# Operand addresses, PSUM banks, the start of the program and the order tables changed in an attention and two-MoE kernel

## The chip, the cores and the metric

The kernel runs on one core of a Trainium2 chip. The metric is the device time of one execution in microseconds (us); lower is better. The median of three timed runs of the kernel before is 945.14 us, with 944.86 and 945.75 as the lowest and the highest. One further execution was profiled; every row below comes from it. Engines are named as in the profile: PE (matmul), PEld (weight load), DVE (vector), ACT (scalar), POOL, SP (starts the DMAs).

## The reference, cut to what matters

```python
# q, k, v: 4 batches x 8 heads x 576 x 64; omega: 128 x 64; x becomes 2304 x 512
def phi(x):                                   # x: q or k, scaled by D ** -0.25
    h = einsum('bhsd,md->bhsm', x, omega) - sum(x * x, -1, keepdims=True) / 2
    return exp(h - max(h, -1)) / sqrt(128)
kv = einsum('bhsm,bhsd->bhmd', phi(k), v);  z = sum(phi(k), 2)
attn = einsum('bhsm,bhmd->bhsd', phi(q), kv) / (phi(q) . z + 1e-6)
x = attn rearranged to 2304 tokens x 512
h = maximum(x @ w_in, 0);  x = (h * h) @ w_out              # moe:  512 -> 2048 -> 512
xn = x / sqrt(mean(x * x) + 1e-6) * rms_g                    # moe2: 512 -> 1536 -> 512
g = xn @ w_gate;  out = (silu(g) * (xn @ w_val)) @ w_out
```

## The kernel before, in words

The work is cut into tokens blocks of 512 columns, one for each of the four batches, and a remainder block (REM) of 4 x 64 tokens that is 256 columns wide. Attention of a batch runs as four pairs of heads. Features (line 661) multiply 64-row halves of the array (form 64*128); products with values and with the kv state (lines 706, 720, 723, 780, 785, 810) use 64-column halves (128*64); transposes (774, 819) use the whole array, as do all large matmuls. The first MoE is `moe1(j)`: for each of 16 chunks of the hidden dimension `hpart` (line 895) multiplies x by w_in into a bank of class `h`, ACT and others form the squared relu, and `ypart` (line 926) adds the product with w_out into four banks that stay accumulating. The second MoE uses `product` (line 1204) and lines 1306, 1326 and 1400. Large matmuls hold fp32r values split in a high and a low part and take three products for each one; each instruction has 512 columns (256 for REM). The program holds 3162 such matmuls of 512 columns and 672 of 256.

Every piece of work is a node in `Plan`, with an engine, a planned duration and the buffers that it reads and writes. `Plan.run` (lines 286 to 312) issues the nodes one after the other in the sequence of the table ORDER. Its words are two bytes: the node's number and, in the top four bits, which of its alternative engines it takes. The word 0xFFFF issues a filler instead (lines 562 to 567): two 256-column matmuls of `ones` by `ones` into an accumulator bank that nobody reads. The table PLACES gives, for each buffer acquired, its class and slot. Work is issued in this order to each engine's own queue, and each engine runs its queue in order, waiting where data or a buffer is missing. DMAs run on SP's queue by `dma` (line 470).

PSUM has eight banks in three classes: `t` (three), `h` (one), `acc` (four). A buffer names the classes that it may take; `banks` in `attention` is `["t"]` for batches 1 to 3. SBUF tiles come from pools; `const`, then `common`, are allotted from one side, `edge` and the attention pool from the other. The weights of moe1 are split once, by `prepare`, during moe1(0), and parts are kept in DRAM (`w1d`).

At the start, ones are set by DVE, fillers begin on PE, and omega is loaded twice (the two 64-row halves), scaled by ACT at line 573 to `oms`, and the row norms of q, k and the remainder are formed (lines 584, 615). Line 668 takes the maxima of features from PSUM on DVE, line 680 the exponentials on ACT.

Of the kernel before, what the change touches and what calls it, by code (L numbers as in the profile page):

```python
# [21 lines left out]


ORDER = bytes.fromhex(
    "000000150005101600170001000400070014ffffffffffffffffffffffffffffffffffffffffffffffffffffffffffff0019"
    "0003002120220023004f0020ffffffffffffffffffffffffffff00240072107320500051001a001b0009000a001c001d001e"
    "001fffffffffffffffffffff000d004e00250074002600270028100b0029004400450043000e000fffffffffffffffffffff"
    "ffffffffffffffffffffffffffffffff0047002a0030000c003600100011001300080012007d0046007e0031004200520048"
    "0049004a004b007f0053004d007c0037004c002e102f00540018002b0180018300a0002c102d0055005c0181005600580057"
    "00801182105d019100710081008201ae10a10059005a00ab009f01840083105b008400860032003301920038003900640185"  # L30
    "00e50065003a003400aa005e009e00cd01a1005fffffffff0075018601af0085119301b01187003b003500760060006100b8"
    "10b9ffffffffffff008c006600ac00a300770194006200a20063008d0078006710e60079008a007a019500680196008b007b"
    "00a4009200a500d801a400ad01a20197007001beffffffff00aeffffffffffff008700a600a700af0069119800b011a300b1"
    "0093008800e401a500b200a901a60089003dffff003c00a8008e008f01b101b2003e003f00b3009400900095009100ce0040"
    "00b40096009700d900b500b600e801a70099009c00da10b700ba00e700c000bb11a801ca00cc00e900980041ffffffff00bc"
    "009d00c100c201b300bd01c1006b01bf00c300be01b40189006e00c400bf00c5006f11b5ffffffff00c700ea010400eb00ec"
    "01c000ca10cf006a00dc00ee006c0162018a018b00cbffff018c018d018e01da01c200dd01c301cb00d001db11dc00de00db"
    "01c411c500df01cc013800e001cd019900e1019a019b019c01ce01e7118f01cf012d019d006d019e01dd019001e811e900e3"
    "00ed009a01de01b701b801df0139213a01d001d101b901ba01ab00d100d200d301e011e1119f009b01ea00e201d301eb01ec"
    "01d401d501f601f901f701ed010200d400d501aa01fa11f801fb0203020401d601ee01d200d700d601ad2105020601a001ac"  # L40
    "01ef020701fc00f2020500f311fd01bb041010f400ef0213021610f000f101c7021402081215021701f001f104710103013b"
    "021f0218020911bc01bd01f200f500f6022f01c9010e0220020a02191472022100f7010600f801c80222020c01c6021a00f9"
    "023001d70223022400fa020d11d801d902320231010f111001e501120225023c0158020e024b00fb00fd020b010002330234"
    "01e402351159023d12260111025801e30490020f01130114015a1236023f01e60201012c011501f30228022901160188024c"
    "0118024e020211f40240123e02410117022a01ff02420200024f0268124d02500107010111f5027412430108010902511252"
    "021012110212022b021b0269021c025b02440245026b0246025c010a012e026c010b010d0259010c125a025d021d025e021e"
    "126a01e2011c0119026d04730275011e00fc111a023a125f022c02760239023b015700fe00ff027704910247023800c6011d"
    "0278011b022d04920284011f122e0248026102910262026302790120012300c800c901210122026e027a01fe126f013c027b"
    "0292028512490257028702880286015601240254129302a00264013d0289013e013f028a02940140112f028b02950296124a"
    "014102970255025602980163027d0130027e02a1027f01b60406027202700142013102a3012502a41164028012a202651266"  # L50
    "02c90273027c013202ad02b002a502a6028c0271029902ae029a029b02811282013301340135013601270267028e02900137"
    "028d029c12af026002b102b202b3012a014602a702ca12cb028302b4028f02ab02bd140702cc02a902c00148022702be12bf"
    "02c102c202c302cd02ce041d029d02aa040802c402d902da01430147023701a9014502b6129e012b02b70144014902b802cf"
    "12d0016502e602db02dc014a014b02ac02b502b902e902f5014c016602d202ba02dd02de029f02c702e7014d02df014e02ea"
    "12e012bb014f02c802d3016701680169016a02e802f8016b016c02c502f612f702d4015b02eb01500312031302f902c6035d"
    "135e02bc02e202fa015c02ec12ed0351035f02e3043c0152015d02fb02fc015e02e402d1030202d502d603500153141e12d7"
    "0305015f031e02ee02530352016002ef043d016102f002e512d8030302fd03060368032102ff13040170016d043e0307032e"
    "0322031f1320030802f102f2030b030c12f30309035c117203151171016f015104b70323016e01730388030d031401540316"
    "031703600318235313190174033b01750301015501770331030004c60176038602fe04d70324030e0361035401780179017b"
    "030a02f4031c13250362031a0363017e04b8017f03640365033e032f03bc030f0367131004b904ba04bb041f033c03920366"  # L60
    "033d0332133003330334033f0369035503270356035703580359035b032803b204cb03400341035a031b0329032a031d0586"
    "1311133503370342136a036b032b036c036d0126132c132d036e036f037005870338037204bf04c023b304c10371033a0588"
    "0345034a03390589058a058b04c20347039303962394012804cc04cd058c058d039504ce03970398038704bc14bd14be0399"
    "039a03e6039b039c138903360129034e059105920344058e0376037703bd058f0346059003b4137803730593037504c30594"
    "05950596034b04c404eb0599038a034c14c504cf038b038c038d038e038f04c904f003740598041113be0597034804ca03bf"
    "059a059b059c039004d804c704d304d50391032604c804d4017a017c017d04df141204d003b1059d059e14d1059f05a0039d"
    "139f139e03e70379037a037b037c14d2041c04d913e8037d050405a205a404d6037e037f04da03a013a204e103b003e904db"
    "04dc14dd04e203b503b603b703a104e405a103b804e504e603b903ba03bb04de05a305a505a604e003a3038003a403a703a8"
    "03dc0447038204e3038304ec03db04ee05ad04e704e814e905a705a805a903c703c9044603a903a503a603c004f104ea03c1"
# [1521 lines left out]
```

## Time and profile before

| | us |
|---|---|
| median of three runs | 945.14 (944.86 to 945.75) |
| the profiled execution | 944.95 |
| its span | 943.1 |
| PE busy | 937.4 (99%) |
| DVE busy | 726.9 (77%) |
| ACT busy | 514.8 (55%) |
| POOL busy | 119.1 (13%) |

The profiled execution lies 0.19 us below the median, and 1.85 us above its own span. Busy time of a matmul group counts from the first start to the last modelled end, so the distance from one start to the next row's start tells the pace. In a timeline, "x3" folds three instructions of one form into a row; attention's fp32 matmuls stand twice each in the trace, so a feature group of eight in the order is x16 there. The granted TensorE clock (PEclk) is 1.00 in most of the span; in the first 6 us the fillers start about 0.21 us apart and after that 0.12 us apart.

### The profile page before, as it was taken

To read this page: it belongs to the slowest core of one execution; us is meant where nothing else is said; L and a number is where in the kernel's file an instruction comes from. 1 tells how busy PE (TensorE), PEld (TensorE's weight loads), DVE (VectorE), ACT (ScalarE), POOL (GpSimd) and SP (SyncE) were. 2 spreads that over 40 slices of the span, in tenths; PEclk is the share of its full clock that TensorE was granted. 3 is DMA by queue.
4 is the path that set the end of the run, shared out by engine and by line. 5 is a ranking of instruction groups with operands and counts; after the bars stand their busy time and mean duration, and the time that the engine had idled before them with its cause. 6 is when DMAs were issued, how large, how long until landed. Compare 5 with 4: busy or idle time off the path is not lost.

```text
span 943.1 us, 16522 instructions
## 1 busy us (share of the span) xinstructions
PE 937.4 (99%) x6132; PEld 787.0 (83%) x6132; DVE 726.9 (77%) x1341; ACT 514.8 (55%) x1080; POOL 119.1 (13%) x107
## 2 busy tenths in 40 slices
PE   9999999999999999999999999999999999999998
PEld 8978878888888888888899888888888888888886
DVE  7999898867666799887878777888998637566565
ACT  5998887655676676544335657544443423333320
POOL 1313322200121001101021011000020101110020
PEclk9999999999999999999999999999999999999999
DMA  8768898898878867757898543243232323112113
GB/s 265 258 214 280 270 310 316 284 296 311 304 262 270 262 233 264 257 193 277 298 307 299 177 140 122 68 152 124 74 104 79 101 77 91 57 57 79 45 34 112
DMA packets 78385, 182.11 MB, mean 193 GB/s; under 512 B 9184, under 2 KB 13408, under 8 KB 78304
## 3 DMA queue, kind: packets, MB, share of 16 engines
q1 hardware_dynamic: 78304, 181.06, 57.8%
q8 instruction: 48, 0.79, 0.3%
q14 instruction: 33, 0.27, 0.1%
HBM read 142.49 MB, written 38.54 MB: 192 GB/s over the span
## 4 chain that ended last, share of the span: by engine, by line
PE 99%; DVE 1%; issue 0%; ACT 0%; DVEq 0%
PE acc L1204 21%; PE acc L926 12%; PE h L895 12%; PE t L1400 12%; PE t L1204 8%; PE acc L1326 5%; PE h L1204 4%; PE h L1400 4%; PE t L661 3%; PE t L1326 3%; PE h L1306 2%; PE acc L564 2%; PE t L720 2%; PE t L1306 1%; PE t L780 1%; PE t L774 1%
## 5 line engine op out<-in xcount | busy, mean ns | idle before, releaser
L1204 PE MATMUL acc<-x,wq 128*128 128x512 f32 x452 | 159.1, 390 | 0.0
L1204 PE MATMUL acc<-xa,wq 128*128 128x512 f32 x350 | 129.7, 389 | 0.0
L1222 DVE TENSOR_TENSOR cc<-acc,cc 128x512 f32<-128x512 f32 x118 | 79.4, 685 | 63.6 <-PE acc L1204 62.5
L1400 PE MATMUL t<-wq,ub 128*128 128x512 f32 x372 | 101.3, 390 | 0.0
L1204 PEld LDWEIGHTS acc<-x,wq 128*128 128x128 f32 x452 | 84.9, 188 | 17.2
L926 PE MATMUL acc<-g,wr 128*128 128x512 f32 (+1 forms) x396 | 89.2, 361 | 0.0
L1400 PEld LDWEIGHTS t<-wq,ub 128*128 128x128 f32 x372 | 69.5, 188 | 14.7 <-DVE wq L476 0.4
L485 ACT CAST wq<-wq 128x512 fp32r<-128x512 f32 x108 | 64.1, 618 | 28.0 <-DMA wq<-w2d4o 10.8
L476 DVE TENSOR_TENSOR wq<-wq 128x512 fp32r<-128x512 f32 x108 | 75.3, 709 | 4.8 <-ACT wq L485 4.6
L1204 PEld LDWEIGHTS acc<-xa,wq 128*128 128x128 f32 x350 | 65.7, 188 | 13.4
L926 PEld LDWEIGHTS acc<-g,wr 128*128 128x128 f32 x396 | 65.0, 189 | 10.5
L680 ACT ACTIVATE p<-t,sm 128x128 f32<-128x128 f32 x220 | 61.6, 398 | 19.7 <-DVE sm L673 14.5
L895 PE MATMUL h<-x,wr 128*128 128x512 f32 x264 | 69.1, 399 | 0.7 <-ACT f L910 0.7
L1408 DVE TENSOR_TENSOR oa<-t,oa 128x512 f32<-128x512 f32 x67 | 45.2, 683 | 17.4 <-PE t L1400 17.2
L895 PEld LDWEIGHTS h<-x,wr 128*128 128x128 f32 x264 | 47.9, 188 | 11.7 <-ACT f L910 1.1
L668 DVE TENSOR_REDUCE sm<-t 128x4 f32<-128x512 f32 x62 | 40.6, 684 | 20.9 <-PE t L661 20.7
L523 ACT ACTIVATE dw<-st 128x512 f32<-128x512 f32 x57 | 39.4, 696 | 15.2 <-DMA w2d4v<-dw 4.5
L528 DVE SCALAR_TENSOR_TENSOR dw<-dw,st 128x512 uint32<-128x512 uint32 x57 | 41.7, 735 | 2.8 <-ACT st L517 1.7
L1381 ACT ACTIVATE cc<-cc 128x512 f32<-128x512 f32 x36 | 22.3, 628 | 37.5 <-DVE cc L1222 37.5
L926 PE MATMUL acc<-g,wu 128*128 128x512 f32 (+1 forms) x180 | 42.6, 362 | 0.0
L910 ACT ACTIVATE f<-h 128x512 f32<-128x512 f32 (+1 forms) x48 | 25.6, 533 | 29.4 <-PE h L895 27.7
L1400 PE MATMUL t<-wq,g 128*128 128x512 f32 x126 | 41.2, 390 | 0.0
(346 smaller groups left out, 2053.6 us busy)
## 6 DMA issues: line engine op xcount, KB each, us to landing
wr<-w1d SPq DMA_DIRECT2D x70, 512.0 KB, 5.6
st<-in_w_out_dram SPq DMA_DIRECT2D x28, 512.0 KB, 4.8
w1d<-wr SPq DMA_DIRECT2D x22, 512.0 KB, 6.5
st<-in_w_in_dram SPq DMA_DIRECT2D x16, 512.0 KB, 5.4
st<-in_w_gate_dram SPq DMA_DIRECT2D x12, 512.0 KB, 4.7
st<-in_w_val_dram SPq DMA_DIRECT2D x12, 512.0 KB, 5.3
st<-y SPq DMA_DIRECT2D x18, 256.0 KB, 4.3
v<-in_v_r_dram SPq DMA_DIRECT2D x16, 260.0 KB, 4.4
```

Source lines behind the costliest of these rows:

```text
L476: return lambda: en.tensor_tensor(out=lo(), in0=src(), in1=f32(hi()), op=ALU.subtract)
L485: first = plan.add("ACT", act(n), prio, lambda: nc.scalar.copy(out=hi(), in_=src()), rd, [whi], after, pre=[blo] if blo is not bhi else [])
L528: lambda: nc.vector.scalar_tensor_tensor(out=out().bitcast(U32), in0=out().bitcast(U32), scalar=3, in1=half(st.ap, 0), op0=ALU.logical_shi ...
L668: lambda fp=fp, js=js: nc.vector.tensor_reduce(out=mx.ap[:, js], in_=fp.ap, op=ALU.max, axis=AX),
L680: nc.scalar.activation(out=pbuf.ap[:, j, :], in_=fp.ap[:, i, :], func=AF.Exp, bias=mx.ap[:, j:j + 1])
L895: nc.tensor.matmul(hb.ap[:, :n], lhsT=u.ap[:, wl, kk * P:(kk + 1) * P], rhs=xcols(j, xl, kk)(), start=(gi == 0 and ii == 0), stop=(gi == l ...
L926: nc.tensor.matmul(accs[e].ap[:, :n], lhsT=u.ap[:, w, es], rhs=x.ap[:, :n], start=(c == 0 and i == 0), stop=(c == C1 - 1 and i == 2))
L1204: nc.tensor.matmul(bank.ap[:, cols], lhsT=u.ap[:, wl, c0 + kk * P:c0 + (kk + 1) * P], rhs=x[kk][xl].ap[:, :cols.stop - cols.start], start= ...
L1222: lambda: nc.vector.tensor_tensor(out=out.ap, in0=bank.ap, in1=x.ap, op=ALU.add), [bank, x], [out])
L1326: nc.tensor.matmul(bank.ap, lhsT=us[dc].ap[:, wl, es], rhs=gs[dc, j][xl].ap, start=dc == i == 0 and (j == 1 or first), stop=dc == 1 and i ...
L1400: nc.tensor.matmul(o.ap, lhsT=x[xl].ap[:, c0:c0 + P], rhs=us[f"o{i}"].ap[:, wl, :], start=i == n == 0, stop=i == 1 and n == 2)
L1408: lambda: nc.vector.tensor_tensor(out=oa.ap, in0=o.ap, in1=oa.ap, op=ALU.add), [o, oa], [oa])
```

## The change

It has five parts.

1. The tile `edge` grows from 8 to 56 columns, and the one-column tile `eps_sb` becomes a slice of a tile `small` of 24 columns. In the program as built the operands of all 3834 large matmuls begin 192 bytes past a multiple of 256 bytes before, and at a multiple of 256 after. `ones` stays 128 bytes past one, and attention's tiles move too.
2. A buffer that may take a bank of one PSUM class may take any of the eight.
3. Omega's two DMAs go through ACT's queue instead of SP's, `oms` is made by DVE instead of ACT, and a one-column Exp into `warm` is added on ACT.
4. The planner's cost of a DMA is at least 0.45, and the first three weight units of moe1 are due 10 units earlier (FIRST, AHEAD).
5. ORDER and PLACES are new. ORDER has 3775 words instead of 3809, and 21 of them are fillers instead of 56: 42 filler matmuls instead of 112. All other matmuls are the same in number. PSUM copies move between engines: 382 on ACT instead of 376, 36 on DVE instead of 42. DVE has 785 TENSOR_TENSOR instead of 777, POOL 94 instructions instead of 99.

Lines below 470 move by 8 to 11: line 661 is 672 after, 895 is 906, 926 is 937, 780 is 791, 564 is 572.

```diff
 ORDER = bytes.fromhex(
-    "000000150005101600170001000400070014ffffffffffffffffffffffffffffffffffffffffffffffffffffffffffff0019"
...
 
 
@@ -222,6 +223,8 @@
 
 
     def __init__(self, classes=None, view=None, ap=None):
+        if classes and classes[0] in BANKS:
+            classes = [*classes, *(c for c in BANKS if c not in classes)]
         self.classes = classes
         self.view = view
         self.ap = ap
@@ -351,6 +354,8 @@
     BLK = [NB] * B + [B * SR]
     REM = B
     LONG = 1
+    FIRST = 3
+    AHEAD = 10.0
     ALONE = 3
     GATE = 11
     PAIR = 2
@@ -365,7 +370,7 @@
     common = ctx.enter_context(tc.tile_pool(name="common", bufs=1))
     psum = ctx.enter_context(tc.tile_pool(name="psum", bufs=1, space=PSUM))
     edge = ctx.enter_context(tc.tile_pool(name="edge", bufs=1, side="right"))
-    edge.tile([P, 8], F32, name="edge")
+    edge.tile([P, 56], F32, name="edge")
     ph1_stack, att_stack, w1s_stack = ExitStack(), ExitStack(), ExitStack()
     ph1 = ph1_stack.enter_context(tc.tile_pool(name="ph1", bufs=1))
     att = att_stack.enter_context(tc.tile_pool(name="att", bufs=1, side="right"))
@@ -427,7 +432,8 @@
     om2 = const.tile([P, M], F32, name="om2")
     oms = const.tile([P, M], F32, name="oms")
     g_sb = const.tile([P, KC], F32, name="g_sb")
-    eps_sb = const.tile([P, 1], F32, name="eps_sb")
+    small = const.tile([P, 24], F32, name="small")
+    eps_sb, warm = small[:, :1], small[:, 1:2]
     v_t = [att.tile([P, 2, R, D + 1], F32, name=f"v{i}") for i in range(2)]
     vr_t = att.tile([P, H * (D + 1) + 8], F32, name="vr")[:, :H * (D + 1)].rearrange("p (h n) -> p h n", h=H)
     kv_t = [att.tile([P, 2, 80], F32, name=f"kv{i}")[:, :, :D + 1] for i in range(2)]
@@ -464,9 +470,11 @@
     def pe(n, cnt, passes=1):
         return cnt * passes * max(0.109, 0.0133 + n / 2400.0)
 
-    def dma(prio, outap, inap, nbytes, r=(), w=(), after=()):
+    def dma(prio, outap, inap, nbytes, r=(), w=(), after=(), act_queue=False):
+        if act_queue:
+            return plan.add("ACT", 0.6, prio, lambda: nc.scalar.dma_start(out=outap(), in_=inap()), r, w, after, tail=2.3)
         return plan.add(
-            "SP", nbytes / 311e3, prio,
+            "SP", max(0.45, nbytes / 311e3), prio,
             lambda: nc.sync.dma_start(out=outap(), in_=inap()), r, w, after, tail=2.5,
         )
 
@@ -565,12 +573,15 @@
                              rhs=ones.rearrange("p (o n) -> p o n", o=1).to_broadcast([P, 2, P]), start=True, stop=True)
 
     plan.filler = Buf(["acc"]), filler
-    b_om = Buf(ap=om2)
+    b_om, b_warm = Buf(ap=om2), Buf(ap=warm)
     for h in range(2):
-        dma(T0, lambda h=h: om2[h * D:(h + 1) * D, :], lambda: omega_t, 32768, w=[(b_om, h)])
+        dma(T0, lambda h=h: om2[h * D:(h + 1) * D, :], lambda: omega_t, 32768, w=[(b_om, h)], act_queue=True)
+    plan.add("ACT", 1.4, T0 + 1.0, lambda: nc.scalar.activation(out=warm, in_=f32(ones[:, :1]), func=AF.Exp), [b_late],
+             [b_warm], after=plan.nodes[-1:])
     dma(T0 + 30, lambda: g_sb, lambda: rms_g.rearrange("(k p) -> p k", p=P), 2048, w=[b_g])
 
-    plan.add("ACT", 0.4, T0, lambda: nc.scalar.activation(out=oms, in_=om2, func=AF.Copy, scale=SCALE), [b_om], [b_oms])
+    plan.add("DVE", 0.2, T0, lambda: nc.vector.tensor_scalar(out=oms, in0=om2, scalar1=SCALE, scalar2=None, op0=ALU.mult),
+             [b_om], [b_oms])
 
     def copy(prio, out, src, n, rd, wr):
 
@@ -866,7 +877,7 @@
                 ring.append([u])
             if j == 0:
                 lo_eng = "ANY"
-                last_split[:] = [prepare(pos, 8.08, ((w_in, w_out)[kind], c), u, lo_eng, last_split + gate)]
+                last_split[:] = [prepare(pos, 8.08 + AHEAD * (i < FIRST), ((w_in, w_out)[kind], c), u, lo_eng, last_split + gate)]
                 if kept(c):
                     w1[i] = u
                 else:
```

SP's queue at the start, before (ld are row-major q, k or remainder rows, om is omega, tr and tt are transposed ones):

```order
1 L470 DMA ld_199<-in_rest_r_dram 128x512
2 L470 DMA om_76<-in_omega_t_dram 64x128 x2
3 L470 DMA tr_211<-in_rest_t_dram 128x512
4 L470 DMA ld_255<-in_q_r_dram 128x512
5 L470 DMA ld_260<-in_q_r_dram 128x512
6 L470 DMA tt_262<-in_q_t_dram 128x512
```

and after; omega's two DMAs stand first on ACT's queue now:

```order
1 L478 DMA tt_199<-in_q_t_dram 128x512
2 L478 DMA ld_236<-in_q_r_dram 128x512
3 L478 DMA lt_239<-in_q_t_dram 128x512
4 L478 DMA tr_241<-in_rest_t_dram 128x512
5 L478 DMA ld_254<-in_q_r_dram 128x512
6 L478 DMA ld_285<-in_rest_r_dram 128x512
```

The transposed first block of q moves from sixth to first place, and the remainder's rows from first to sixth.

PE's queue at the start, before (L564 is the filler):

```order
1 L564 MATMUL acc_197<-ones 128x256 x30
2 L661 MATMUL acc_243<-oms,tr_211 128x128
3 L661 MATMUL t_244<-oms,tr_211 128x128
4 L661 MATMUL acc_243<-oms,tr_211 128x128
5 L661 MATMUL t_244<-oms,tr_211 128x128
6 L661 MATMUL acc_243<-oms,tr_211 128x128
7 L661 MATMUL t_244<-oms,tr_211 128x128
8 L661 MATMUL acc_243<-oms,tr_211 128x128
9 L661 MATMUL t_244<-oms,tr_211 128x128
10 L564 MATMUL acc_197<-ones 128x256 x14
```

and after, from the first filler (L572) to the second feature group:

```order
1 L572 MATMUL acc_197<-ones 128x256 x16
2 L672 MATMUL acc_225<-oms,tt_199 128x128
3 L672 MATMUL t_226<-oms,tt_199 128x128
4 L672 MATMUL acc_225<-oms,tt_199 128x128
5 L672 MATMUL t_226<-oms,tt_199 128x128
6 L672 MATMUL acc_225<-oms,tt_199 128x128
7 L672 MATMUL t_226<-oms,tt_199 128x128
8 L672 MATMUL acc_225<-oms,tt_199 128x128
9 L672 MATMUL t_226<-oms,tt_199 128x128
10 L672 MATMUL t_243<-oms,lt_239 128x128
```

Behind the last row of this piece stand two more groups of eight and then a filler of 6. Before, each of the first four groups of L661 has a filler of 10 to 30 ahead of it; after, the first three groups follow each other, and the fillers are 16, 6, 12, 2, 4 and 2.

PE's queue in moe1(0), before (L895 and L926 are large matmuls, L780 and L785 attention's products, L661 features):

```order
475 L895 MATMUL h_2018<-x_1009,wr_1928 128x512
476 L780 MATMUL t_2030<-kv_83,qt_1933 64x65 x8
477 L785 MATMUL t_2030<-kv_83,qr_1989 64x65 x2
478 L780 MATMUL t_2031<-kv_83,qt_1934 64x65 x8
479 L895 MATMUL h_2018<-x_817,wr_1928 128x512
480 L895 MATMUL h_2018<-x_982,wr_1928 128x512
481 L895 MATMUL h_2018<-x_915,wr_1928 128x512
482 L895 MATMUL h_2018<-x_1008,wr_1928 128x512
483 L926 MATMUL acc_1226<-g_1890,wr_1870 128x512
484 L926 MATMUL acc_1226<-g_1891,wr_1870 128x512
485 L926 MATMUL acc_1226<-g_1890,wr_1870 128x512
486 L661 MATMUL t_2079<-oms,tt_1031 128x128
```

and at a place of the same kind after (L791 and L796 are L780 and L785, L672 is L661, L937 is L926):

```order
919 L791 MATMUL h_3317<-kv_83,qt_3276 64x65 x8
920 L796 MATMUL h_3317<-kv_83,qr_3197 64x65 x2
921 L791 MATMUL t_3318<-kv_83,qt_3277 64x65 x8
922 L672 MATMUL t_3346<-oms,tt_2933 128x128
923 L672 MATMUL t_3347<-oms,tt_2933 128x128
924 L672 MATMUL t_3346<-oms,tt_2933 128x128
925 L672 MATMUL t_3347<-oms,tt_2933 128x128
926 L672 MATMUL t_3346<-oms,tt_2933 128x128
927 L672 MATMUL t_3347<-oms,tt_2933 128x128
928 L672 MATMUL t_3346<-oms,tt_2933 128x128
929 L672 MATMUL t_3347<-oms,tt_2933 128x128
930 L937 MATMUL acc_2805<-g_3161,wr_2998 128x512
```

Before, the products and the features are each set between large matmuls by themselves; after, the features follow directly on the products. Over the whole program PE goes from a 64-wide form back to a 512-column matmul 43 times before and 29 times after; it goes from one 64-wide form to the other directly 12 times before and 20 times after.

## Rows read from the trace of the kernel before

**Rows 1.** The page: span, and busy time of each engine.

```profile
span 943.1 us, 16522 instructions
PE 937.4 (99%) x6132; PEld 787.0 (83%) x6132; DVE 726.9 (77%) x1341; ACT 514.8 (55%) x1080; POOL 119.1 (13%) x107
```

**Rows 2.** The page: chain that ended last, share of the span by engine.

```profile
PE 99%; DVE 1%; issue 0%; ACT 0%; DVEq 0%
```

**Rows 3.** PE's waits for other engines behind the first: total, times, longest.

```profile
PE h L895 <- ACT f L910: 0.7, 1, 0.7
PE t L1204 <- DVE cs L1222: 0.2, 1, 0.2
```

**Rows 4.** Timeline of PE, large matmuls in a row: start, us, engine, line.

```profile
700.92 0.84 PE L1400 MATMUL t<-wq,g 128*128 128x512 f32 x3
701.60 0.84 PE L1400 MATMUL t<-wq,ub 128*128 128x512 f32 x3
```

**Rows 5.** Timeline of PE, 256 columns between 512 columns.

```profile
472.89 1.12 PE L895 MATMUL h<-xr,wr 128*128 128x256 f32 x8
473.84 0.40 PE L1326 MATMUL t<-gs,wu 128*128 128x512 f32 x1
```

**Rows 6.** Timeline of PE, attention's 64-row matmuls between large ones, and their steady pace.

```profile
7.57 0.27 PE L661 MATMUL acc<-oms,tr 64*128 64x128 f32 x1
7.68 0.27 PE L661 MATMUL acc<-oms,tr 64*128 64x128 f32 x1
...
57.42 0.84 PE L926 MATMUL acc<-g,wr 128*128 128x512 f32 x3
58.19 1.16 PE L661 MATMUL t<-oms,tt 64*128 64x128 f32 x16
59.28 3.02 PE L895 MATMUL h<-x,wr 128*128 128x512 f32 x12
62.14 2.20 PE L926 MATMUL acc<-g,wr 128*128 128x512 f32 x9
```

**Rows 7.** Line 564, the fillers: count, duration min/median/max, first and last start.

```profile
L564 PE MATMUL acc<-ones x112: 276/283/582, 1.1 to 48.9; 128*128 128x256 f32 x112
```

**Rows 8.** Timeline of PE in the first 17 us.

```profile
1.05 6.15 PE L564 MATMUL acc<-ones 128*128 128x256 f32 x30 [1.05 <-DVE ones L548]
7.13 0.37 PE L661 MATMUL acc<-oms,tr 64*128 64x128 f32 x1
8.22 1.94 PE L564 MATMUL acc<-ones 128*128 128x256 f32 x14
16.97 1.16 PE L661 MATMUL acc<-oms,tt 64*128 64x128 f32 x16
```

**Rows 9.** Timeline of the other engines in the first 8 us.

```profile
0.74 0.40 SPq L470 DMA_DIRECT2D ld<-in_rest_r_dram  x1
1.20 1.20 SPq L470 DMA_DIRECT2D om<-in_omega_t_dram  x2
3.06 0.91 SPq L470 DMA_DIRECT2D ld<-in_q_r_dram  x2
3.63 0.63 ACT L583 ACTIVATE ld<-ld 128x512 f32<-128x512 f32 x1 [1.62 <-DMA ld<-in_rest_r_dram]
4.17 0.30 ACT L573 ACTIVATE oms<-om 128x128 f32<-128x128 f32 x1
4.29 0.69 DVE L615 TENSOR_REDUCE sm<-ld 128x8 f32<-128x512 f32 x1 [3.30 <-ACT ld L583]
6.06 0.69 DVE L584 TENSOR_TENSOR ld<-ld 128x512 f32<-128x512 f32 x1 [1.08 <-DMA ld<-in_q_r_dram]
```

**Rows 10.** Timeline of PE, the first transposes behind a large matmul.

```profile
46.46 0.60 PE L819 MATMUL t<-ident,xw 128*128 128x128 f32 x4
```

**Rows 11.** Busy time by stretch: PE, PEld, DVE, ACT, POOL, PEclk, DMA, GB/s.

```profile
0.00:46.46 46.46, 45.41 (x662) 41.74 (x663) 38.72 (x100) 35.74 (x104) 10.58 (x15) 1.00 0.78 261
0.00:100.00 100.00, 98.26 (x1096) 84.25 (x1096) 87.49 (x202) 84.63 (x212) 26.88 (x27) 1.00 0.77 254
```

More of the change, by code (lines that the diff above doesn't have):

```diff
@@ L20 @@
 EXP_HI = float.fromhex("0x1.dffffep+32")
+BANKS = ["t", "h", "acc"]
 ORDER = bytes.fromhex(
[L25 to L28 removed]
@@ L29 @@
[L29 to L33, printed above, removed]
@@ L174 @@
[L174 to L177 removed]
+    "0000004f00030001000400050008ffffffffffffffffffffffffffffffff0053005020510021001500250022102300520054"
+    "00550056005700580026002700240028001a0016101700290018000affffffffffff000e001b0059002a000b001c002b0044"
@@ new lines @@
+    "001d100c001e000f0010000d0011ffffffffffffffffffffffff00311032019200120193001f00200045003700380013ffff"
+    "0048001420460047004901950072000900730076002f007700740194004a001901960030ffffffff002c002d002effff0033"
+    "0181004b004c004d00750184018200780034007d0081007900390035004301a2005d00a1004e00e60197007a0082007e0071"
+    "007b005e005a00a000360185118300ab003a008b0083007c0186005f0060006501a301af107f003b11a410a200800084005b"
+    "0088006600890085018700ac003c00a4005c00e5008c0061108a00a3003d00a5006200a61188019811990067006300cd00a7"
@@ new lines @@
+    "00860087006800af00a8003f01b001a5006400930069008d00b000ad00d9006a00b100b900a901b2009f00ae0040008e00aa"
+    "006b00e7006c00b200b301a6006d008f00ba0094006e009500b500e800b600b7009001bf003e00b401a701b300bb01c011b1"
+    "009101a801b4009200b811a900c1006f00700041004200e9010f00bc00ea01b501cb00de00bd009600c200c3015811b600eb"
+    "00ec01c101c200da009700ed019a00be009800c400ee00c500bf018a01c300c000c600ef01cc01c4009a009d019b00c8009e"
+    "01ce00cb018b018c00df01c511c601db00cc10db01b800e000dc01cd01de00cf018d018e018f119000ce01cf20d001df01dc"
@@ new lines @@
+    "018901d001d111dd00e101e801e0019c019d0110016301b9013a01ba01d2019e01d401e9019f00e201eb00e4111101d501e1"
+    "019121a001d600d101a111ea0099009b009c01f700c711e2011200d201b701bb00d3010300e301f800d401ac01ec01ed01d7"
+    "00c900ca0204113b00d501fa01fb00d601f901fc01c801ee01ef00d701ae01ab01c701ad01fd00dd00f301640205010401ca"
+    "1206020702080209021401f001f100d800f501c911fe020a013c0165020b01d801bc00f010f211bd10f10105110602170220"
+    "023001be022100f4022301f201ff021811d901f3020d04910007021512160219023d0224022201da02310225021a022601e5"
@@ new lines @@
+    "01e700f600f700fa020e01e6024c020f121b0232000200fb00fc016600f800f91227023301e40107023e0234023501f40113"
+    "022911f50202021002400236011401150116022a01170241023f0237022b024201f60203024f012f02501492024d02280200"
+    "0118124e02510259025a047202430244020102111212021f011901080109010a02691213021e010b010c125b021d025c025d"
+    "025e024501d314730252022c021c027502530493020c041d02850239010d012d025f0260026c1130026d0159026a022d126b"
+    "122e023b026e023c0276010e01390246023a011d02470292022f026f12700278011a02570248013104070474028602550277"
@@ new lines @@
+    "0279012e0287111b027a028802a1025602620263027b111f027c0293011e0289129402580249124a02640448028a1408024b"
+    "011c0120029502610296029702650121013d0122012301240272028b02ae128c027e02661267027f013e013f0298014002a4"
+    "028001250254028d14490141014202a212a3012602710273029902af026802a502a60143013201aa02b1029002b002b202b3"
+    "02a712a80274029102ca02810133013402be02b401350136013802cd02e702cb12cc0282028f029a029b115a02b502b702ce"
+    "02cf02da02bf1283028412c002c1028e013702c2029c029d00fe010102b802c302ab02e8015b014702c4010212c502b90409"
@@ L218 @@
+    "0803000008090582400780438207090581010204060180414040420a00080003064301050207828203044101820340820140"
+    "80028240820005018083420a01410106074083400181838202"
 )
```

340 lines of the change are left out of this document (159 added, 181 removed).

## The prediction

> **What bounds the kernel now.** I read the page's busy times first, then the chain of waits, PE's waits, its timeline, and last the start of the program. PE is busy 937.4 of 943.1 us [rows 1], and the chain that ended last is PE for 99% [rows 2]. Behind the first filler PE waits for another engine for 0.9 us in all by the view of waits [rows 3]. So an edit matters only where it changes the number of matmuls, the distance between their starts, or what PE does while it has nothing to do. The last is hidden in the busy share: 112 fillers, whose products nobody reads, run until 48.9 us [rows 7].
>
> PE's time divides as follows. Three 512-column matmuls start 0.68 us after the three before [rows 4], which is 226.7 ns each; 512 columns at the granted clock of 1.00 [rows 11], which is 2.4 GHz, take 213.3, so 13.3 ns lie between. Eight of 256 columns take 0.95 us [rows 5], 119 ns each, and 106.7 plus 13.3 is 120. The fillers, taken from the start of each run to the next real matmul, take 17.5 us in all; the longest is 1.05 to 7.13 us, 30 of them at 0.20 us, the next 14 take 8.22 to 10.09 less their 0.1 [rows 8]. The rest is the real matmuls, about 920.5 us, with some 4 us of small stalls inside, the first microsecond, and about 4 us between the last matmul's start and the end.
>
> **The change part by part.** The sum is made against the profiled execution, 944.95 us, which is its span of 943.1 [rows 1] and 1.85 around it; the median of the timed runs lies 0.19 above.
>
> *Fewer changes of form.* A visit to a 64-wide form costs PE more than its matmuls. The row at 57.42 us holds three matmuls and the next starts 0.77 later, where three take 0.68 [rows 4, 6]: 0.09. The 8 pairs of features behind it take 58.19 to 59.28, 1.09 us, where the pace of a pair is 0.11 (7.57 to 7.68), so 0.88: 0.21. The twelve large ones after that take 2.86 to 62.14, where twelve take 2.72: 0.14. Together 0.44 us for going and coming back [rows 6]. The order returns 43 times from a 64-wide form to 512 columns before and 29 after: 14 less, -6.2 us. In exchange eight more direct changes between the two 64-wide forms, each at the 0.1 to 0.2 that one change costs in these rows: +0.8 to +1.6. I take -4.8. The bounds are -6.2 and -3.4 (14 times the 0.35 without part of the inner cost, less 1.5).
>
> *The start.* Fillers fall from 112 to 42. At the rate of 0.20 us the first 16 end at about 4.3 us instead of 7.1, and 26 at 0.12 to 0.14 take 3.4: 6.6 us of fillers instead of 17.5. But a filler stands where PE would wait anyhow, so what counts is who is waited for. That is DVE: from the start to the transposes at 46.46 us [rows 10] it is busy for 38.72 us, in 100 instructions, and idle for 7.74 [rows 11]. Counting the new order's instructions ahead of the first large matmul, with the same durations, DVE has 95 instructions and 0.3 us less to do. So the start is shorter by what DVE idles less. Of the 7.74 us, 4.1 lie ahead of its first reduction at 4.29 and 1.08 ahead of 6.06, where it waits for a block of q [rows 9]. The first DMA to be used took from its issue at 0.74 to 3.63, 2.9 us; two were issued within 0.9 from 3.06 on [rows 9]. Afterwards q's two blocks come first and second on SP's queue, at about 0.74 and 1.15, and omega on ACT's queue, so the first data are there at about 3.7 to 4.1 in both programs; what goes is the wait at 6.06 and much of the small ones that follow, because features are ready at about 5 and not 8 us. I expect DVE to idle about 5 us instead of 7.74: -2.7, with the lesser work -3.0. The bounds are 0, when DVE's waits only move, and -5.5, when it idles only until its first data.
>
> *ACT afterwards.* AHEAD and the new order bring the splitting of the first weights forward, and six more PSUM copies fall to ACT. Up to 100 us ACT is busy for 84.63 [rows 11], that is idle for 15.4. Adding up ACT's instructions in queue order with the durations of before, 82.3 us of ACT's work stand ahead of the products of line 780 that PE reaches with 78.6 us of its own work done; after, 89.0 stand ahead of such products (line 791) with 82.3 done. PE is then at about 99.5 us, if the 20.2 us by which it lies behind its own work there (first microsecond, fillers, waits) shrink by 3. So ACT may idle for 10.5 us at most until then. An earlier start gives it some 2.5 to 3 of the five that it lacks; the rest must come out of waits behind 10 us. I take +1.0, from 0 to +6.2 (89.0 + 15.4 less 98.2, no idle time saved).
>
> *Addresses.* No large matmul of the trace begins at a multiple of 256 bytes: all 3834 are 192 past it, so the new case is not shown. The fillers' operands are 128 past one, and their pace, 0.12 us in the run to 16.97 and 120 ns by the formula of the 256-column row, is the same as that of 192 past [rows 5, 8]. A cost of crossing lines should differ between 512 and 256 columns or between 128 and 192 bytes; 13.3 ns is the same in all three. So I take zero. The bounds are +0 and the whole gap: 13.3 ns x 3834 = -51 us; a loss has no row for it, since 128 and 192 agree.
>
> The Trainium skill, "TensorE: Matmul & The Clock Gate", section "Wait — 56ns, not 53.3ns?", gives a warm matmul as its columns at 2.4 GHz and a fixed 2.5 ns, 215.7 ns for 512. By that the pace here would have 10.8 ns to lose, 41 us over the large matmuls, and the time would be about 896 us. The trace disagrees for the kernel as it is, 226.7 against 215.7 [rows 4]; no run here shows whether the addresses are the cause.
>
> *Banks, omega, oms, warm.* That any buffer may take any bank lets the order above be, and could spare the wait of 0.7 us for line 910, where `h` has one bank [rows 3]: -0.7 at best, which I leave inside the range. Omega's two issues take 1.2 us on SP [rows 9] and now run on ACT ahead of its table load, while ACT idles until 3.63; oms costs DVE 0.3 at most, counted above. They are hidden by the wait for the first block; without that cover they cost their 1.2. The copies moved from DVE to ACT lie behind PE elsewhere in the program, where ACT is at 55% and DVE at 77% [rows 1].
>
> Sum: 944.95 - 4.8 - 3.0 + 1.0 = 938.15, and 0.19 more on the median's scale: 938.3. I say 938, with an own range of 932 to 943.5.
>
> **The rivals.**
>
> *All the room is used.* PE waits neither in the start nor on ACT: DVE idles only until its first data (-5.5), the form changes give -6.2, the wait on line 910 goes (-0.7), and 2 to 3 us of small stalls go with it. That is 944.95 - 12.4 - 2.5 = 930. For it: 70 fillers less, 8.4 us at 0.12. Against it: DVE's sum of 36.6 us cannot be passed. Chance 0.17.
>
> *The gap between large matmuls shrinks.* If the 13.3 ns are a matter of where an operand begins, all 3834 get faster; half of it is 25 us, all of it 51: 887 to 913 with the other terms. Against it speak the equal gaps at 128 and 192; for it only that no row has offset zero. Chance 0.09, middle 905.
>
> *No net change.* The saved form changes are paid back by waits for ACT of 4 to 6 us: 943.3 to 946. Chance 0.10.
>
> *Slower.* ACT is late at the products and features that PE reaches with 82 to 84 us of its work done. If ACT idles as before, PE stands for 6.2 us there, without fillers to cover it. The clock, which in the first 6 us gave fillers at 0.20 instead of 0.12 us [rows 8], would fall in such a wait; while it is back at half speed some 5 us of time do 2.6 us of work, so another +2.6, and a second such wait in the next pair as much again. With no gain in the start: 944.95 - 4.8 + 6.2 + 2.6 = 949. It decides when ACT's idle time up to 98 us is above 14 us and the start gains nothing; ACT's 10 us of idle time in its first 20 speak for it, that its p exponentials start earlier speaks against. Chance 0.09.
>
> **How the numbers follow.** The forecast has 0.55, the full room 0.17, the gap 0.09, no change 0.10, slower 0.09. A change within 0.2%, 1.9 us, is what a measurement of this kernel cannot tell from none. The forecast's own range ends under 943.2 nearly everywhere, so faster has 0.55 + 0.17 + 0.09 = 0.81, same 0.10, slower 0.09. For 8 in 10 I leave out the gap below and half of the slower case above: 927 to 946.
>
> **What would show it.** The pace of the 512-column rows: 226.7 says that the addresses did nothing, 216 that they did. The first large matmuls and the transposes of 46.46 us [rows 10]: about 3 us earlier if DVE's idle time fell as I say; DVE's idle time up to there, 5 us. PE's waits between 90 and 110 us for ACT: about 1 us, over 6 in the slower case, with PEclk below 1.00. Distances in a visit as before, 0.44 us each. I am wrong if large matmuls start at another distance, if the start is not shorter, or if ACT's lateness shows a wait of more than 3 us.

## The result and the profile after

The changed kernel takes 936.67 us, the median of six runs from 934.23 to 938.64; beside it the kernel before took 945.44. The ratio is 0.9905, with a 95% interval of 0.9887 to 0.9922: 8.8 us faster, 938 forecast. The profiled execution is the fastest of the six, 934.23 us, so its 10.7 us under the profiled 944.95 of before are more than the typical gain.

The page of the changed kernel, its span, busy times and chain by engine:

```profile
span 932.4 us, 16368 instructions
PE 923.7 (99%) x6062; PEld 778.6 (84%) x6062; DVE 718.4 (77%) x1341; ACT 516.5 (55%) x1086; POOL 111.0 (12%) x102
PE 94%; ACT 4%; DVE 1%; DMA 0%; issue 0%; ACTq 0%; DVEq 0%
```

PE is still the bound, but ACT now has 4% of the chain that ended last, where before PE had 99% [rows 1, 2]. All of that lies in the first 67 us, as shown below. The distance of large matmuls has not moved: three from 699.87, and as before 0.68 us to the next row [rows 4].

```profile
699.87 0.84 PE L1215 MATMUL t<-x,wq 128*128 128x512 f32 x3
700.55 0.39 PE L1215 MATMUL acc<-xa,wq 128*128 128x512 f32 x1
```

PE's waits behind the first by name, total, times and longest; four more, of 0.2 to 0.3 us each, are for ACT:

```profile
PE t L672 <- ACT pr L691: 1.0, 1, 1.0
PE t L785 <- DVE sm L769: 0.8, 1, 0.8
PE acc L672 <- DVE oms L583: 0.5, 1, 0.5
PE acc L717 <- DVE xw L770: 0.4, 1, 0.4
```

They are 3.7 us where before there were 0.9 [rows 3], and the wait of a large matmul for ACT is gone. What a page of 99% busy hid is seen in the fillers: 112 of them [rows 7] took 17.5 us, 42 now take 10.1. PE's time from the first start to the last divides in fillers, 17.47 and then 10.06, and real matmuls with the waits between them, 920.46 and then 917.09. These two differences, 7.4 and 3.4, are the gain of the profiled run (938.98 to 928.21 for the last matmul's start).

The start after, PE's rows of the fillers and first features, and the first large matmuls:

```profile
1.05 3.79 PE L572 MATMUL acc<-ones 128*128 128x256 f32 x16 [1.05 <-DVE ones L556]
5.35 0.37 PE L672 MATMUL acc<-oms,tt 64*128 64x128 f32 x1 [0.51 <-DVE oms L583]
...
41.88 0.96 PE L906 MATMUL acc<-x,wu 128*128 128x512 f32 x3
```

Features start at 5.35 instead of 7.13 us [rows 8]. The first large matmul starts at 41.88; before it was this row:

```profile
45.20 0.95 PE L895 MATMUL h<-x,wr 128*128 128x512 f32 x3
```

That is 3.3 us. How far PE lies behind its own work tells the rest. Count each real matmul at the pace that it has inside a group in these traces: 226.7 ns for 512 columns, 120 for 256, 109 for a transpose on the whole array, 58.6 for a pair in the two 64-column halves, 112 for a pair in the two 64-row halves. That makes 893.7 us of work in both kernels; all else is lateness. With 24 us of work done, about where the large matmuls begin, PE was 21.4 us late before and is 17.5 late now; with 36 done (60.5 us of time before, 54.0 now), 24.4 and 17.9; at the end 45.2 and 34.5. So of the 10.8 us the start gives 6.5, 4.0 of it up to the first large matmuls and 2.5 right behind them. The other 4.3 come later. Visits to a 64-wide form, set between 512-column matmuls, cost 14.4 us above that pace behind the start before, and 9.9 after: that accounts for them.

Busy time by stretch, of before and then of the changed kernel (columns as in the rows ahead: PE, PEld, DVE, ACT, POOL, clock, DMA share, GB/s):

```profile
0.00:50.00 50.00, 48.95 (x684) 44.37 (x686) 42.15 (x108) 38.81 (x112) 10.58 (x15) 1.00 0.75 250
```

```profile
0.00:50.00 50.00, 45.25 (x641) 39.55 (x642) 43.87 (x113) 43.50 (x125) 11.09 (x15) 1.00 0.84 276
20.00:50.00 30.00, 28.14 (x448) 24.28 (x448) 29.21 (x80) 29.92 (x87) 8.88 (x7) 1.00 0.81 269
0.00:100.00 100.00, 95.15 (x1050) 79.52 (x1052) 91.22 (x212) 91.45 (x225) 21.04 (x24) 1.00 0.85 277
```

Up to 50 us ACT idled for 11.2 us before and for 6.5 now; DVE for 7.9 and 6.1. From 20 to 50 us both are nearly full now. Up to 100 us ACT idles for 8.6 us, where it idled for 15.4 [rows 11].

Which of the two PE waits for is read from the chain that ended last, its start (start, us, what):

```profile
1.31 3.65 DMA om<-in_omega_t_dram
...
5.07 0.24 DVE oms L583
...
8.33 1.14 ACT p L691 x4
...
35.38 0.69 PE acc L791 x16
...
66.43 0.64 ACT f L594
...
67.09 0.70 DVE g L484
...
67.84 1.43 PE acc L937 x5
```

It goes from omega's load over oms and the features to ACT, stays on ACT's queue from 8.33 to 35.3 us, mostly line 691, the exponentials, and goes over to PE at 35.38. It leaves PE once more, from 51.4 to 67.8 us, for ACT and DVE with weights, exponentials and the squared relu; from 67.84 on it stays on PE. The two stretches hold 25.8 and 11.4 us of ACT, the 4% of the page. The second costs PE little: its matmul at 67.84 starts 0.49 us behind the one before and the next 0.34 behind that, 0.37 more than the pace.

### The profile page after: what moved, and what is told of

It reads as the page before. It is cut to its first block, busy times and chain, and to the rows that moved or that the text cites. A ratio compares the mean times of both kernels' runs of the same rounds, so it can differ in the third digit from the quotient of the medians.

```text
span 932.4 us, 16368 instructions
## 1 busy us (share of the span) xinstructions
PE 923.7 (99%) x6062; PEld 778.6 (84%) x6062; DVE 718.4 (77%) x1341; ACT 516.5 (55%) x1086; POOL 111.0 (12%) x102
## 4 chain that ended last, share of the span: by engine, by line
PE 94%; ACT 4%; DVE 1%; DMA 0%; issue 0%; ACTq 0%; DVEq 0%
PE acc L1215 15%; PE t L1215 13%; PE acc L937 11%; PE t L1411 7%; PE acc L1411 6%; PE acc L1337 5%; PE h L1215 5%; PE t L906 5%; PE h L906 4%; PE t L1337 3%; PE t L672 3%; PE acc L906 2%; PE h L1411 2%; ACT p L691 2%; PE t L1317 1%; PE acc L1317 1%
## 5 line engine op out<-in xcount | busy, mean ns | idle before, releaser
L1215 PE MATMUL acc<-x,wq 128*128 128x512 f32 x314 | 105.9, 390 | 0.0
L937 PE MATMUL acc<-g,wr 128*128 128x512 f32 (+1 forms) x363 | 84.7, 367 | 0.1
L1233 DVE TENSOR_TENSOR cc<-acc,cc 128x512 f32<-128x512 f32 x73 | 49.4, 686 | 38.0 <-PE acc L1215 37.6
L937 PEld LDWEIGHTS acc<-g,wr 128*128 128x128 f32 x363 | 61.5, 189 | 11.2 <-DVE g L484 0.5
L1215 PE MATMUL acc<-xa,wq 128*128 128x512 f32 x183 | 69.7, 390 | 0.0
L1215 PE MATMUL t<-x,wq 128*128 128x512 f32 x189 | 64.4, 390 | 0.0
L1411 PE MATMUL t<-wq,ub 128*128 128x512 f32 x215 | 58.8, 389 | 0.0
L531 ACT ACTIVATE dw<-st 128x512 f32<-128x512 f32 x55 | 39.1, 713 | 16.5 <-DMA st<-in_w_val_dram 10.4
L1215 PE MATMUL t<-xa,wq 128*128 128x512 f32 x125 | 48.0, 390 | 0.0
L1411 PEld LDWEIGHTS t<-wq,ub 128*128 128x128 f32 x215 | 40.2, 188 | 8.2
L1411 PE MATMUL acc<-wq,ub 128*128 128x512 f32 x162 | 45.5, 389 | 0.0
L679 DVE TENSOR_REDUCE sm<-t 128x4 f32<-128x512 f32 x52 | 34.5, 683 | 13.1 <-PE t L672 11.7
L1215 PEld LDWEIGHTS t<-x,wq 128*128 128x128 f32 x189 | 35.3, 188 | 7.1
L1215 PEld LDWEIGHTS acc<-xa,wq 128*128 128x128 f32 x183 | 34.4, 188 | 6.9
```

Of the source, the lines that this page charges most:

```text
L531: lambda: nc.scalar.activation(out=out(), in_=hf(), func=AF.Abs, scale=65536.0), [(st, 1)], [w])
L679: lambda fp=fp, js=js: nc.vector.tensor_reduce(out=mx.ap[:, js], in_=fp.ap, op=ALU.max, axis=AX),
L937: nc.tensor.matmul(accs[e].ap[:, :n], lhsT=u.ap[:, w, es], rhs=x.ap[:, :n], start=(c == 0 and i == 0), stop=(c == C1 - 1 and i == 2))
L1215: nc.tensor.matmul(bank.ap[:, cols], lhsT=u.ap[:, wl, c0 + kk * P:c0 + (kk + 1) * P], rhs=x[kk][xl].ap[:, :cols.stop - cols.start], start= ...
L1233: lambda: nc.vector.tensor_tensor(out=out.ap, in0=bank.ap, in1=x.ap, op=ALU.add), [bank, x], [out])
L1411: nc.tensor.matmul(o.ap, lhsT=x[xl].ap[:, c0:c0 + P], rhs=us[f"o{i}"].ap[:, wl, :], start=i == n == 0, stop=i == 1 and n == 2)
```

## The experiments

The letters are those of the texts written ahead of each run. Theory A is the prediction's: the start and fewer changes of form made the gain, and the addresses none. All times are medians beside runs of the kernel before on the same chip; the groups ran on different chips, so across groups the ratios are compared.

**The changed kernel again, the addresses in both directions, and the old start.**

> The changed kernel once more, as the yardstick of this group, since its six times spread over 4.4 us (934.2 to 938.6) where the kernel before spreads over 2.1. Theory A (start and fewer form changes made the gain): 936.7, between 934 and 939, 512-column pace 226.7 ns, and the profile shows the spread in the first 60 us, where PE now waits between fillers. Rival B (the addresses made part of it): the same time; the two part in the next runs.

> The changed kernel with its large operands 192 bytes past a multiple of 256 again, all else as in it. Theory A: within 1 us of the changed kernel, about 937, and the same 226.7 ns. Rival B: slower by what the addresses gave, 1.4 us if only the slow starts over 229 ns come back (4.3 instead of 2.8 us of excess), up to 5 if the growth of the gap between large matmuls does.

```diff
-    edge.tile([P, 56], F32, name="edge")
+    edge.tile([P, 8], F32, name="edge")
-    small = const.tile([P, 24], F32, name="small")
+    small = const.tile([P, 8], F32, name="small")
```

> The kernel before with its large operands at multiples of 256 bytes, all else as before. Theory A: 945.4 within 1 us, ratio 1.000. Rival B: faster by 1.4 to 5 us, 940 to 944.

```diff
-    edge.tile([P, 8], F32, name="edge")
+    edge.tile([P, 56], F32, name="edge")
-    eps_sb = const.tile([P, 1], F32, name="eps_sb")
+    eps_sb = const.tile([P, 24], F32, name="eps_sb")[:, :1]
```

| | us | ratio to before (95%) |
|---|---|---|
| changed kernel again | 935.29 | 0.9895 (0.9882 to 0.9909) |
| its operands 192 bytes past | 935.31 | 0.9894 (0.988 to 0.9907) |
| before, operands at 256 | 945.69 | 1.0006 (0.9997 to 1.0015) |

The addresses do nothing, in either kernel. Nor do they touch the slow starts: 512-column matmuls over 229 ns are 416 before, 449 with the new addresses, 345 and 363 in the two traces of the changed kernel, 339 with the old addresses. Theory B falls. Timelines of PE, first with the old addresses in the changed order, then with the new ones in the order before; three matmuls take 0.68 us in both:

```profile
700.38 0.84 PE L1215 MATMUL t<-x,wq 128*128 128x512 f32 x3
701.06 0.39 PE L1215 MATMUL acc<-xa,wq 128*128 128x512 f32 x1
```

```profile
700.95 0.84 PE L1400 MATMUL t<-wq,ub 128*128 128x512 f32 x3
701.63 0.62 PE L1400 MATMUL t<-wq,g 128*128 128x512 f32 x2
```

The run of the changed kernel also shows where some of its spread lies: in omega's landing. DVE's timeline there:

```profile
6.02 0.23 DVE L583 TENSOR_SCALAR oms<-om 128x128 f32<-128x128 f32 x1 [5.03 <-DMA om<-in_omega_t_dram]
```

In the first profile DVE got omega at 5.07 us, here at 6.02, with the old addresses at 5.61; the spans are 932.4, 933.7 and 933.0. Matmul by matmul the delay of 0.9 us at 5 us is still 0.9 at 217 us. The start of the changed kernel has no slack.

> The changed kernel with omega on SP's queue and oms by ACT again; its tables, addresses and the rest stay. Omega's two issues then stand ahead of q's first block on SP, 1.2 us. Theory A: the first features start 0.5 to 1.5 us later (5.9 to 6.8 us instead of 5.35), and since DVE is the one waited for up to 50 us, the whole program ends as much later: 937.2 to 938.2. Rival C (the start's data are not what the first 50 us wait for, only the sum of DVE's and ACT's work is): no difference, 936.7.

```diff
-        dma(T0, ..., 32768, w=[(b_om, h)], act_queue=True)
+        dma(T0, ..., 32768, w=[(b_om, h)])
-    plan.add("DVE", 0.2, T0, lambda: nc.vector.tensor_scalar(out=oms, ...
+    plan.add("ACT", 0.4, T0, lambda: nc.scalar.activation(out=oms, in_=om2, func=AF.Copy, scale=SCALE),
```

936.40 us, ratio 0.9906 (0.9892 to 0.992): 1.1 above the changed kernel, inside both intervals. So omega's queue and oms are worth about 1 us at most. With the addresses at nothing, 8 us or more are left for the order of the work, with the banks and the planner's costs that came with it; these were not run apart. Its profiled run, 937.93, started features at 5.58 us, 0.23 later than the changed kernel's first profile, and lost another 3 us by 39 us: about 1 early on, about 1 in a wait of 1.7 us for DVE, where the changed kernel waits for 0.8, and about 1 right behind it, while the granted clock was 0.50, its lower level, from 36.4 to 39.8 us. The other three runs took 936.2 to 936.5, so part of that belongs to this one run.

**The fillers left out.**

> The changed kernel without its 42 fillers, which take 10.1 us of PE's time by its trace. Theory A (fillers stand where PE waits for DVE and ACT anyway): the waits take their place, the time stays at 935.5 within 1.5 us as long as the clock stays full; where PEclk falls in the first 20 us the cost is up to 3 us. Rival D (fillers delay the real matmuls): faster by 3 us or more, 932.

> The kernel before without its 112 fillers, which take 17.5 us of PE's time. Theory A: the time stays at 945.5 to 949, since DVE's queue of 38.7 us up to 46 us sets when PE goes on. Rival D: faster by 7 us or more, because 70 fillers less is what the change saved; about 938.

```diff
             if w == 0xFFFF:
-                self.filler[1](filled)
                 continue
```

935.37 us (0.9896, 0.9881 to 0.991) and 944.71 us (0.9992, 0.9983 to 1.0002). Neither moves by more than 0.5 us. A filler takes the place of a wait, and the 70 fillers less are a sign of the gain, not its cause; theory D falls. Nor does the time depend on the clock there: without fillers PE of the kernel before was busy for 0.8 of the 3 us from 12 to 15 us, and from 15.2 to 18.6 the granted clock was 0.50, where it is 1.00 with fillers. The waits that come out from under the fillers of the kernel before name what its start waited for, first three blocks in a row, then ACT in five waits that were not seen with fillers, 2.4 us:

```profile
PE acc L660 <- DMA tr<-in_rest_t_dram: 5.6, 1, 5.6
PE acc L660 <- DMA tt<-in_k_t_dram: 1.8, 1, 1.8
PE acc L660 <- DMA tt<-in_q_t_dram: 1.0, 1, 1.0
```

In the changed kernel without fillers it is omega (4.9 us), then ACT's exponentials. The chain of the same run:

```profile
3.52 4.38 DMA ld<-in_q_r_dram
...
7.93 0.70 DVE ld L583
...
11.03 2.15 ACT pr L679 x8
```

So before, loads held the start up to there: DVE's queue has the squares of two blocks of q's rows ahead of the first maxima. They were issued fifth and sixth on SP's queue, DVE could take the second at 7.93 us, and ACT's first exponentials started at 11.03. In the changed kernel the first of these blocks is issued second, the second goes to ACT, and the exponentials start at 8.33. From 11 us on ACT and DVE share the chain of before. That the order of these loads alone would give the gain was not run; it is read from the chain.

**DVE or ACT.**

> The changed kernel with DVE's sums for the row norms of batch 0 taken over an eighth of each row (10 instructions of 0.69 us become short ones, about -5.5 us of DVE's work in the first 35 us). Theory A (DVE sets the length of the start): faster by 3 to 5 us, 931 to 932.5. Rival E (ACT, which is busy for 10.0 of every 10 us from 10 to 60, sets it): within 1 us of 935.5.

```diff
-  in_=x.ap, op=ALU.add
+  in_=x.ap[:, :, :8] if b == 0 else x.ap, op=ALU.add
```

> The changed kernel with the four exponentials of each feature bank of batch 0 taken in one instruction with the first one's bias (about 0.4 to 0.5 us less for each of 18 banks, -8 us of ACT's work in the start). Theory A (DVE sets the length of the start): within 1 us of 935.5. Rival E (ACT sets it): faster by 4 us or more, under 931.5.

Both kernels leave out work that the result needs (most of the row sums, three of four maxima) and serve for their time only.

```diff
                     def ex(fp=fp, js=slice(*places[h])):
+                        if b == 0:
+                            nc.scalar.activation(out=pbuf.ap[:, js, :], in_=fp.ap, func=AF.Exp,
+                                                 bias=mx.ap[:, js.start:js.start + 1])
+                            return
```

DVE lighter: 935.80 us (0.9905, 0.9889 to 0.9922). Matmul by matmul it is the same within 0.13 us up to 217 us, though DVE does 3.2 us less by 60 us. So DVE is not what the start of the changed kernel waits for, and my claim on that falls. ACT lighter: 936.35 us (0.9905, 0.9891 to 0.992), with 8.5 us less of ACT's work by 60 us. No gain either, but the chain has changed: between 5 and 50 us it stood on ACT for 25.8 us in the changed kernel, and here on DVE for 35.0, on ACT for none. PE was 0.42 us ahead by 23 us, though its features had started 0.78 later, and 1.95 behind by 42 us, with new waits for DVE:

```profile
PE t L795 <- DVE xw L774: 1.1, 1, 1.1
```

So ACT sets the start, with DVE so close behind that 8 us less of ACT's work buy nothing.

> The changed kernel with both lighter: DVE's row sums of batch 0 over an eighth of each row, and ACT's four exponentials of a bank in one. Alone, neither moved the time. Theory G (DVE and ACT are both full from 10 to 60 us and take turns in setting the length of the start): now faster by 3 us or more, 932 or less. Rival H (the loads set it, or the order itself): within 1.5 us of 935.5.

Both edits together: 934.44 us (0.988, 0.9865 to 0.9895). By the ratios that is 1.4 to 2.4 us under the changed kernel (0.9895 and 0.9905 in its two groups), but the intervals overlap, and the time lies in the range of rival H. In the trace PE was 1.8 us ahead by 34 us, though its features started 0.4 later; it was 0.8 ahead by 42, and 0.1 behind by 217. So theory G is right in that both have to be lighter for the start to move, and wrong in the size. The chain from 5 to 50 us is now PE's own work for 34.4 us and loads for 5.7, of which 5.4 a block of w_out, as rival H said, and the lead is lost again, most of it in a wait of 0.8 us for an exponential at 175 us. The next bound stands right behind the two.

**The price of a visit.**

> The changed kernel with a visit to a 64-wide form put in on purpose: two small matmuls of ones by ones, in the two column halves, ahead of each of the 87 six-matmul products of 512 columns that open a bank in the second MoE; their result is overwritten by the product. Theory A (a visit costs PE 0.3 to 0.45 us beside its matmuls): together with the matmuls themselves, four passes of about 0.055 us, 0.5 to 0.65 us each, +44 to +57 us, and more than the control below by 20 us or more. Rival F (a change of form costs nothing; the rows read as its price are waits for buffers): as the control, within 5 us.

> The control: the same two small matmuls at the same 87 places in the whole-array form (128 columns of weights instead of 64). Theory A: four passes of 0.05 to 0.11 us each, +17 to +38 us. Rival F: the same time as the visits.

```diff
         def mm():
+            if first and cols == ALL:
+                for cs in HALVES:
+                    nc.tensor.matmul(bank.ap[cs, :64], lhsT=f32(ones)[:, cs], rhs=f32(ones)[:, :64], start=True, stop=True)
```

978.51 and 977.64 us: 43 and 42 us more than the changed kernel's 935.3, about 0.49 for each of the 87. By time alone the two are the same, as rival F said; the 20 us between them that theory A wanted did not come, and 978.51 lies just under A's range. The control was badly made: its own matmuls cost more than I had put down, so the two times decide nothing. PE's timeline at one place of the first kernel and the same place of the control:

```profile
726.76 0.85 PE L1414 MATMUL t<-wq,g 128*128 128x512 f32 x3
727.54 0.34 PE L1215 MATMUL t<-ones 128*64 128x64 f32 x4
727.81 0.73 PE L1218 MATMUL t<-x,wq 128*128 128x512 f32 x2
728.38 0.40 PE L1218 MATMUL t<-xa,wq 128*128 128x512 f32 x1
```

```profile
724.31 0.86 PE L1414 MATMUL t<-wq,g 128*128 128x512 f32 x3
725.01 0.56 PE L1215 MATMUL t<-ones 128*128 128x64 f32 x4
725.37 0.70 PE L1218 MATMUL t<-x,wq 128*128 128x512 f32 x2
725.92 0.40 PE L1218 MATMUL t<-xa,wq 128*128 128x512 f32 x1
```

In the first, the three large ones take 0.78 to the next row where three take 0.68, the visit 0.27, and the two behind it 0.57 where two take 0.45: 0.49 added. The median of the 75 visits with 512-column matmuls on both sides is 0.47, and 0.46 in the control. In the control the passes follow each other at 0.11, 0.44 of that, so next to nothing is left. The visit's four passes run two and two side by side. At the 58.6 ns that a pair takes in the kernel's longer groups of this form they would be 0.12 of the 0.47, and 0.35 is the price of going and coming: 0.09 ahead of the visit, 0.05 behind its first pair, 0.10 behind its last, 0.11 behind the first large matmul. These distances are the same within 0.01 us at all 75 places, and the view of waits names none of the visits, which speaks against rival F's waits for buffers. So the price is seen in the rows, by the pace that is taken for the passes, and not in the difference of the two times.

**A version with omega on two queues.**

> The changed kernel with omega's first half on SP's queue behind q's first block, and only the second on ACT's. In three runs of the changed order DVE got omega at 5.07, 5.61 and 6.02 us, and the program ended as much later: 932.4, 933.0 and 933.7 us of span. On ACT's queue omega took 3.3 us from issue to landing, on SP's 2.2. Theory A: DVE starts oms at 4.2 to 4.8 us, the first features at 4.85, right behind the fillers, and the span is 931.5 to 932.5, the median 0.5 to 1 us under the changed kernel's, with less spread. Rival: q's rows, now 0.6 us later, hold DVE up instead: no gain or 0.5 us of loss.

```diff
-        dma(T0, ..., w=[(b_om, h)], act_queue=True)
+        dma(T0, ..., w=[(b_om, h)], act_queue=h == 1)
```

934.77 us (0.9888, 0.9874 to 0.9903), not told apart from the changed kernel (0.9895 and 0.9905 in its two groups). DVE got omega at 3.96 us and features started at 4.42, 0.9 earlier, but the next loads were late:

```profile
3.96 0.23 DVE L583 TENSOR_SCALAR oms<-om 128x128 f32<-128x128 f32 x1 [2.96 <-DMA om<-in_omega_t_dram]
5.42 0.69 DVE L595 TENSOR_TENSOR ld<-ld 128x512 f32<-128x512 f32 x1 [1.22 <-DMA ld<-in_q_r_dram]
```

PE's second group of features waited 0.5 us for its load at 6.08, and from 10 us on PE was 0.2 behind the changed kernel's first profile: the rival of the expectation.

## Why the prediction was right, and where not

*Addresses, zero.* Right, and shown both ways. The 215.7 ns for 512 columns of the Trainium skill ("TensorE: Matmul & The Clock Gate", section "Wait — 56ns, not 53.3ns?"), weighed there, is the pace in no trace here, at either address: 226.7.

*Fewer changes of form, -4.8.* Right. Above the pace inside a group, a visit to the features costs 0.40 us in the traces of both kernels, one to the products 0.34 to 0.35, and one to both in a row 0.54; the 0.44 read ahead of the change had some noise of the eleven matmuls behind it. Between 512-column matmuls there were 38 visits before, 15.2 us in all, and there are 24 after, 10.4 us: 4.8 less, of which 4.5 behind the start. A visit to the products in the kernel before, with 18 pairs: the four large ones ahead of it take 1.01 us to the next row, where four take 0.91, and the visit takes 1.20, where 18 pairs take 1.05. The rest, 0.11, lies behind the first large one of the last row:

```profile
69.34 1.08 PE L895 MATMUL h<-x,wu 128*128 128x512 f32 x4
70.35 0.69 PE L780 MATMUL t<-kv,qt 128*64 128x65 f32 x16
70.86 0.29 PE L785 MATMUL t<-kv,qr 128*64 128x65 f32 x4
70.98 0.64 PE L780 MATMUL t<-kv,qt 128*64 128x65 f32 x16
71.55 1.65 PE L926 MATMUL acc<-g,wu 128*128 128x512 f32 x6
```

Starts of 512-column matmuls more than 229 ns apart, away from other forms, add up to 4.3 us over the pace before and 2.8 to 3.0 after. Most of the difference is in the few over 300 ns, 1.7 us before and 0.5 to 0.7 after, among them the wait for line 910; the rest are 2.6 us before and 2.3 to 2.4 after.

*The start, -3.0.* Up to the first large matmuls the size is about right, 3.3 us by time and 4.0 by work done; with the 2.5 right behind them it is more than twice the forecast. The reason, "That is DVE", failed: a DVE with 3 us less to do changes nothing. The chain stands on ACT from 8 to 35 us. Its first exponentials start 2.5 us earlier (10.84 us in the profile of before, 8.33 after), by the chains because one block of q's rows, issued second, stands ahead of DVE's first maxima, and no longer two, issued fifth and sixth. What shrank most is ACT's idle time, by 4.7 us of 50, not DVE's, by 1.7. I had counted DVE's queue ahead of PE and not ACT's, though ACT's had the larger idle time to lose. The signs that I had named, transposes 3 us earlier (43.38 instead of 46.46) and DVE idle for about 5 us up to there (5.7), both came and could not tell the two engines apart; making each lighter could.

*Banks, omega, oms, warm, nothing; 0.7 at best for the wait on line 910.* This term was too small. Before, behind the first large matmuls stand fillers, two visits of features and the wait, which cost 0.96 us with the slow restart behind it. The last filler ends where these rows begin:

```profile
48.98 0.86 PE L895 MATMUL h<-x,wr 128*128 128x512 f32 x3
49.77 1.16 PE L661 MATMUL t<-oms,lt 64*128 64x128 f32 x16
50.86 3.02 PE L895 MATMUL h<-x,wu 128*128 128x512 f32 x12
54.57 2.79 PE L895 MATMUL h<-x,wr 128*128 128x512 f32 x11 [0.69 <-ACT f L910]
```

After, 39 large matmuls in a row, from 44.90 to 53.99 us, write `acc` banks, where every line 895 before writes `h`:

```profile
44.90 3.24 PE L906 MATMUL acc<-x,wr 128*128 128x512 f32 x13
47.98 1.52 PE L906 MATMUL acc<-x,wu 128*128 128x512 f32 x6
49.34 4.72 PE L906 MATMUL acc<-x,wr 128*128 128x512 f32 x20
53.99 0.34 PE L821 MATMUL acc<-ident,xw 128*64 128x64 f32 x4
```

That is the 2.5 us behind the first large matmuls. That the banks allow it is seen in the names; the banks alone were not run.

*ACT afterwards, +1.0.* It came as 0.4, and earlier, at 67.84 us. I had bounded ACT's idle time up to 98 us at 10.5; it was 8.6 up to 100, and PE waits for nothing between 85 and 115 us. The slower rival fell with it.

So in the profiled runs the start gave 6.5 us, where the text had 3.0 and nothing for the banks, and what came behind it 4.3, the changes of form with ACT's 0.4 in it, where the text had 4.8 less 1.0. That run got omega early; the second profile of the changed kernel had 5.5 and 4.0. The forecast of 938 lies 1.3 us above the first median and 2.7 above the second. The term for the form was right; that the sum came so near is partly luck, since the start was sized at less than half and put down to the wrong engine, and the gain between the first medians, 8.8 us, is below the 10.4 of the second.

## What to carry to other kernels

On an engine that is always busy, look for work that nobody reads: fillers mark waits, and leaving them out shows by name what is waited for. Count changes of the matmul's form when ordering small and large ones, and keep small groups together. Where two engines are full, the chain tells which one is waited for, and making each lighter alone and then both tells how far behind the next bound is. An idle time that shrinks as forecast does not show that its engine was the one waited for.

## What was not expected of the hardware

Two loads of 32 KB took 3.3 to 3.7 us (median of the two, three runs) from issue to landing on ACT's queue with large loads beside them on SP's, and 2.2 and 2.4 us on SP's queue (two runs). The time at which DVE got omega varied from 5.07 to 6.02 us between three runs of one order. A visit of four short matmul passes cost 0.35 us beyond their pace in a longer group, about 0.2 of it behind the last pass.
